# Moving the last down-projection gradient slab to the end of a fused forward and backward kernel, with other orders at its start

## The chip, the cores and the metric

The kernel runs as one program on one core of a Trainium2 chip. The metric is device time in microseconds (us) of one execution. Five runs of the kernel before are given, and one more execution under the hardware profiler, whose views are read here. TensorE does the matrix multiplications, VectorE and ScalarE work element by element, GpSimd mostly issues transfers, and SyncE does nothing else. The views call them PE, DVE, ACT, POOL and SP.

## The reference

The input `x` has 2048 rows of 1024 columns. The output is `x + s * g`, with two branches on the normalized rows, and the kernel returns the output and nine gradients.

```python
xn = _layernorm(x)
k_shift = sum(k_pad[t:t+S] * shift_k[:, 3-t])      # four taps
kv = k_shift * v
y = irfft(rfft(kv, 2S) * rfft(ssm_k, 2S))[:S]      # long convolution
y = y + kv * ssm_D
s = xn * y
h = (xn @ w_gate) * (xn @ w_up)                    # 1024 -> 3584
g = silu(h @ w_down)                               # 3584 -> 1024
out = x + s * g
_out, _vjp = jax.vjp(_f, x, k, v, shift_k, ssm_k, ssm_D, w_gate, w_up, w_down)
```

## The kernel before

**Tiles.** The 2048 rows are 16 blocks of 128. The 3584 hidden columns are 14 slabs of 256 (`NSL`, `SLW`). Matrix multiplications accumulate in PSUM, from where ScalarE or VectorE takes them out. The 1024 channels of the convolution are 8 groups of 128 (`ds`) or 4 pairs (`dp`).

**Order.** The program is recorded by a layer that keeps the order of the statements mostly, hoists what has a higher priority, and inserts the waits. Every engine then works through a fixed list, so an instruction that waits holds back what stands behind it on its engine. That holds for the issue of transfers too: SP and POOL have one list each. `tc.issue_after` keeps an instruction behind another one. `make_pump` runs a second stream of work (a generator which yields estimated costs) in pieces between the matrix multiplications, up to a given fraction.

**The stages, by time in the profile.**

1. Start, to about 86 us. `layer_norm` (L533) normalizes six chunks of rows (1, 1, 2, 4, 4 and 4 blocks), mostly on VectorE. The transposed rows go to `XNT`. `gu_unit` (L604) multiplies one chunk with one slab of the gate and up weights: PSUM `psg` (two buffers), then ScalarE's copy `gut` (L618), then on VectorE `hN = gate * up`, then transposes (L636) and `hT`. The order of the first units is a list in the loop over `xs`: units 0 to 3 do slab 0 and then slab 1 of their chunk. In the same loop the four taps of the shift are turned on ScalarE (`turn_taps`, L150, two at a time), spread to all partitions through memory (`WTd`, `Wbc`), and the sine tables are built (`build_tables`, L168, transposes L190, copies to `TI` L191).
2. To about 548 us. The other slabs of the units, with the forward convolution (`conv_forward`, L645) pumped between them. It loads shifted `k` rows and `v` (`load_kv`), multiplies by the taps (`shift`), transposes filter rows loaded by `load_h` (L692 and L694), transforms (L231), multiplies spectra and transforms back.
3. To about 744 us. `h @ w_down` (L1102) and the gate (`gate`, L1107).
4. To about 1368 us. Per slab: `dh` (L1233) and the gradients of the gate and up weights (L1250), with the convolution's gradient (`conv_backward`, L939, beginning with `dy_forward`, L916) pumped between.
5. To 1570 us. The gradient of `w_down`: for each slab `k` a matrix of 256 by 1024, 64 multiplications of 128x512 with depth 2048 (L1353), ScalarE's copies (L1355) and stores. In between SP issues loads for stage 6: transposed weights `WGU` (`load_wgu`, L1314, 14 pieces) and transposed gradients `dgut` (`load_dgut`, L1316, 14 pieces for four blocks of rows). For k = 13 piece 5 is loaded, pieces 6 to 13 follow after that slab's last store.
6. To the end. `dx`: for every block of rows 14 parts (`dx_part`, L1373) of 8 multiplications (L1376), then `ln_backward` (L1393): add the other branch's gradient, two ScalarE passes with row sums into `dx_t` (L1405, L1407), the correction, and the store of `out_1`. `dx_t` has one buffer. Blocks 0 to 3 are done together, then pairs; blocks 14 and 15 one by one, block 15 in two halves of columns. Pumped into this (L1380) is `dk_units` (L1039): 16 units for the gradients of `k` and the taps. A unit takes seven VectorE operations of about 0.7 us and four of about 1.2 us (L1081), and SP loads two transposed tiles for it, `kT` (L1053) and `dkT` (L1055), each with one buffer.

Of the kernel before, what the change touches and what calls it, by code (L numbers as in the profile page):

```python
# [19 lines left out]
def build_kernel(  # L20
# [147 lines left out]
    def build_tables(psp, tg, ang):  # L168

        m = ang  # L170
        for q in range(2):
            dst = T4[q].rearrange("p r k f -> p k r f")
            sc = 2.0 * np.pi / 4096.0
            mm = tg.tile([P, 8, P], I32, name="mm")
            if q == 0:
                V.tensor_single_scalar(mm[:], m[:], 4095, ALU.bitwise_and)
            else:
                nc.gpsimd.iota(mm[:], pattern=[[512 * q, 8], [0, P]], base=0, channel_multiplier=0)
                tt(mm[:], m[:], mm[:], ADD)
                V.tensor_single_scalar(mm[:], mm[:], 4095, ALU.bitwise_and)  # L180
            nc.scalar.activation(dst[:, 1], mm[:], ACT.Sin, bias=negpi[:], scale=sc)
            ab_ = tg.tile([P, 8, P], F32, name="ab_")
            nc.scalar.activation(ab_[:], mm[:], ACT.Abs, bias=negpi[:], scale=sc)
            nc.scalar.activation(dst[:, 0], ab_[:], ACT.Sin, bias=mhpi[:], scale=1.0)
        for j in range(2):
            for rq in range(2):
                ps = psp.tile([P, 4, 2, P], BF16, name="tr")
                for i in range(4):
                    for k in range(2):
                        nc.tensor.transpose(ps[:, i, k, :], T4[j][:, 4 * rq + i, k, :], ident[:])  # L190
                V.tensor_copy(TI[:, j, 4 * rq:4 * rq + 4], ps[:])  # L191
# [320 lines left out]
    for i in range(52):  # L512
        nc.tensor.matmul(ps[:, i % 4, :], ident[:], ident[:], start=True, stop=True)

    bsb = pool("bc_sb", 1)
    tg = pool("tg", 1)
# [128 lines left out]
    def conv_forward():  # L645
        cx = pool("cx", 1)
        cs = pool("cs", 1)
        kst = pool("kst", 1)
        S_ = {}

        def load_kv(dp, c):
            v = U[4][:, 2048 * c:2048 * c + 2048].rearrange("p (a x) -> p a x", a=8)
            cld_v(v, c, dp * 256, 256)
            k = kst.tile([P, 2, 11, P], BF16, name="k", bufs=2)
            for e in range(2):
                cld_k(k[:, e], c, 2 * dp + e)
            S_["kv", dp, c] = (k, v)

# [45 lines left out]
        def tail(ds):  # L704
            G = S_.pop(("G", ds))
            yf = cs.tile([P, NB, P], BF16, name="yf")
            for rp in range(4):
# [5 lines left out]
                yield  # L713

        load_h(0)
        with tc.issue_after(xsts[4].ins):
            load_kv(0, 0)
            load_kv(0, 1)
        def half(ds, x, i, first=None):
# [70 lines left out]
        for _ in tl:  # L790
            yield 1.0
        kst.release()
        cs.release()
        cx.release()

    F_TOTAL = 4 * 20.0 + 6.0 + 8 * (0.5 + FWD4_W + 1.3 + PROD_W + INV_W) + 10.0 - 0.95 * 8 * (4 * 1.75 + 0.95 + 4 * 0.9)
    F_TOTAL += len(EIGHT) * 2 * (FWD8_W - 9.6 + 0.95 * 1.75) - 2.0
    chunks = [(0, 1), (1, 1), (2, 2), (4, 4), (8, 4), (12, 4)]
    xs = [(b0, n, u8((4, 6, 7)[b0 // 4 - 1], a=4) if n == 4 else lnp.tile([P, n, D], BF16, name=f"x{b0}")[:])
# [20 lines left out]
    for i, (b0, n, x4) in enumerate(xs):  # L820
        if i + 1 < len(xs):
            with tc.issue_after(last.ins):
                last, root, xst = layer_norm(*xs[i + 1])
            xsts.append(xst)
        if i in (2, 3):
            with tc.issue_after(act_copy[0].ins):
                for j in (2 * i - 4, 2 * i - 3):
                    turn_taps(j)
        if i == 3:
            with tc.issue_after(xsts[-1].ins):  # L830
                spread_taps()
        for i_, sl in ([(i, 0), (i, 1)] if i < 4 else ([(4, 0)], [(5, 0), (4, 1), (5, 1)])[i - 4]):
            gu_unit(sl, *xs[i_][0:2], slabs[sl], nop)
        if i == len(xs) - 1:
            with tc.issue_after(root.ins), tc.issue_after(last.ins):
                build_tables(ps_st, tg, ang)
    st(RSd.rearrange("(c u r) -> u c r", c=2, u=P), RSTD[:].rearrange("u (c r) -> u c r", c=2))
# [4 lines left out]
    ps_cv = pool("ps_cv", 2, space=PSUM)  # L842
    pump, drain = make_pump(conv_forward(), F_TOTAL)
    cnt = [0]
# [71 lines left out]
    def dy_forward(xs_, sp, cs, then):  # L916
# [10 lines left out]
        load(1)  # L927
        yield 4.0
        half(0, 0)
# [162 lines left out]

    C_TOTAL = 4.0 + 8 * FWD8_W + 16 * (PROD_W + INV8_W) + 8 * 1.4 + 8 * 2.5
    bpump, bdrain = make_pump(conv_backward(), C_TOTAL)

# [220 lines left out]
    def load_dgut(g, n):  # L1316
# [5 lines left out]
        return t  # L1322

    flush()
    ts = []
    for k in range(NSL):
        if k + 2 < NSL:
            load_h(k + 2)
# [13 lines left out]
        if k == 12:  # L1342
            load_wgu(6, gw.tile([P, 4, D], BF16, name="W1")[:])
            ts.append(load_dgut(0, 4))
        if k == 13:
            ts.append(load_dgut(0, 5))
        h = hs.pop(k)
        for f in range(2):
            wbs = wo.tile([P, D], BF16, name="wbs")[:]
            for dh in range(2):  # L1350
                ps = ps_b.tile([P, 512], F32, name="psb")
                for b in range(NB):
                    nc.tensor.matmul(ps[:], h[:, b, f * P:(f + 1) * P], DBM[b // 4][:, b % 4, dh * 512:(dh + 1) * 512],  # L1353
                                     start=(b == 0), stop=(b == NB - 1))
                nc.scalar.copy(out=wbs[:, dh * 512:(dh + 1) * 512], in_=ps[:])  # L1355
# [16 lines left out]

    def dx_part(t, i, ps, n, dhs=(0, 1)):  # L1373
        for f in range(4):
            for dh in dhs:
                nc.tensor.matmul(ps[:, dh * 512:(dh + 1) * 512], t[n][:, f, i * P:(i + 1) * P],  # L1376
                                 WGU[n][:, f, dh * 512:(dh + 1) * 512],
                                 start=(n == 0 and f == 0), stop=(n == 13 and f == 3))
        kcnt[0] += 1
        kpump(kcnt[0] / (14.0 * 14))  # L1380

    ln_in = {}

    def ln_loads(b):
        rows = slice(b * P, (b + 1) * P)
        ts_ = []
        for nm_, src in (("dxna_t", DXNAd), ("xn_t", XNd), ("dout_t", grad_out.flatten_outer_dims())):
            t = gl.tile([P, D], BF16, name=nm_, bufs=1)
            cld(t[:], src[rows, :])
            ts_.append(t)  # L1390
        ln_in[b] = ts_

    def ln_backward(b, mm, parts=1):  # L1393

        rows = slice(b * P, (b + 1) * P)
        dxna_t, xn_t, dout_t = ln_in.pop(b)
        dxn = gl.tile([P, D], F32, name="dxn", bufs=1)
        prod = gl.tile([P, D], F32, name="prod", bufs=1)
        dx_t = gl.tile([P, D], BF16, name="dx_t", bufs=1)
        cols = [slice(h * D // parts, (h + 1) * D // parts) for h in range(parts)]  # L1400
        sums = gs.tile([P, 2, 2], F32, name="sums")
        for h, cl in enumerate(cols):
            ps = mm(h)
            tt(dxn[:, cl], ps, dxna_t[:, cl], ADD)
            nc.scalar.activation(dx_t[:, cl], dxn[:, cl], ACT.Identity, accum_out=sums[:, 0, h:h + 1])  # L1405
            tt(prod[:, cl], dxn[:, cl], xn_t[:, cl], MUL)
            nc.scalar.activation(dx_t[:, cl], prod[:, cl], ACT.Identity, accum_out=sums[:, 1, h:h + 1])  # L1407
        if parts == 2:
            tt(sums[:, :, 0], sums[:, :, 0], sums[:, :, 1], ADD)
        negm = gs.tile([P, 2], F32, name="negm")  # L1410
        pinned(V.tensor_scalar(negm[:], sums[:, :, 0], -1.0 / D, None, op0=MUL))
        for cl in cols:
            nc.scalar.activation(prod[:, cl], xn_t[:, cl], ACT.Identity, bias=negm[:, 0:1], scale=negm[:, 1:2])  # L1413
            tt(dxn[:, cl], dxn[:, cl], prod[:, cl], ADD)
            pinned(V.scalar_tensor_tensor(dx_t[:, cl], dxn[:, cl], RSTN[:, b:b + 1], dout_t[:, cl], op0=MUL, op1=ADD))  # L1415
            if parts == 1:
                ln_loads(b + 1)
            (st if parts == 1 else ld)(out_1.flatten_outer_dims()[rows, cl], dx_t[:, cl])

    for n in range(6, 14):  # L1420
        with tc.issue_after(wst.ins):
# [10 lines left out]
    for i in range(4):  # L1432
# [5 lines left out]
        with tc.high_priority(40):  # L1438
            ln_backward(i, lambda h: pss[i][:])
    for g in range(1, 4):  # L1440
        for b in (4 * g, 4 * g + 2):
            if b == NB - 2:
                break

            pss = [ps_x.tile([P, D], F32, name="psx") for i in range(2)]
            for n in range(14):
                for i in range(2):
                    dx_part(ts, b % 4 + i, pss[i], n)
                if b % 4 == 2:
                    ts[n] = load_dgut(g + 1, n)  # L1450
            for i in range(2):
                with tc.high_priority(40):
                    ln_backward(b + i, lambda h: pss[i][:])
    for b in (NB - 2, NB - 1):
        parts = 2 if b == NB - 1 else 1

        def mm(h):
            ps = ps_x.tile([P, D], F32, name="psx")
            for n in range(14):
                dx_part(ts, b % 4, ps, n, (h,) if parts == 2 else (0, 1))  # L1460
            return ps[:, h * 512:(h + 1) * 512] if parts == 2 else ps[:]
        ln_backward(b, mm, parts)
    kdrain()
    for p_ in (ps_x, kw_, gs, gl, gd2, ub, ua, gd, gw):
# [64 lines left out]
```

## Time and profile before

| what | value |
|---|---|
| five runs: median (lowest to highest) | 1979.06 us (1961.16 to 1982.79) |
| profiled execution: time | 1975.54 us |
| profiled execution: span, first to last instruction | 1973.8 us |
| outside the span | 1.7 us |
| PE busy | 1924.1 us, 97% of the span |
| DVE busy | 1525.5 us, 77% |
| last matrix multiplication of the program | starts near 1960.5 us |
| mean speed, all transfers | 225 GB/s |

The busy time of PE is near the span, so what PE does not fill (about 50 us) is what a new order can move. It has two sorts: waits of PE inside the stages, and the stretch after its last matrix multiplication.

### The profile page before, as it was taken

To read this page: it belongs to the slowest core of one execution; us is meant where nothing else is said; L and a number is where in the kernel's file an instruction comes from. 1 tells how busy PE (TensorE), PEld (TensorE's weight loads), DVE (VectorE), ACT (ScalarE), POOL (GpSimd) and SP (SyncE) were. 2 spreads that over 40 slices of the span, in tenths; PEclk is the share of its full clock that TensorE was granted. 3 is DMA by queue.
4 is the path that set the end of the run, shared out by engine and by line. 5 is a ranking of instruction groups with operands and counts; after the bars stand their busy time and mean duration, and the time that the engine had idled before them with its cause. 6 is when DMAs were issued, how large, how long until landed. Compare 5 with 4: busy or idle time off the path is not lost.

```text
span 1973.8 us, 27333 instructions
## 1 busy us (share of the span) xinstructions
PE 1924.1 (97%) x10907; PEld 1039.4 (53%) x11043; DVE 1525.5 (77%) x1716; ACT 642.2 (33%) x945; POOL 361.3 (18%) x528
## 2 busy tenths in 40 slices
PE   8999999999999998999999999999999999999997
PEld 4555555555444446666556666664444444444443
DVE  8799999999636554888898989999986332666665
ACT  5655555555422234333222222221212101111113
POOL 3413122111112220000122122021212000111111
PEclk9999999999999999999999999999999999999998
DMA  8968667557799988566778778575898999999892
GB/s 283 304 218 271 230 221 262 193 181 254 258 288 287 292 279 271 182 219 207 258 238 275 235 228 284 193 269 178 163 267 215 145 190 218 188 171 179 170 170 77
DMA packets 452271, 444.43 MB, mean 225 GB/s; under 512 B 282656, under 2 KB 370536, under 8 KB 438192
## 3 DMA queue, kind: packets, MB, share of 16 engines
q1 hardware_dynamic: 390976, 228.93, 47.1%
q0 software_dynamic: 44848, 184.39, 28.6%
q10 hardware_dynamic: 16320, 29.36, 4.0%
q8 instruction: 86, 1.41, 0.3%
q14 instruction: 41, 0.34, 0.1%
HBM read 194.00 MB, written 189.84 MB: 194 GB/s over the span
## 4 chain that ended last, share of the span: by engine, by line
PE 59%; issue 14%; DVE 10%; DMA 9%; POOL 3%; SPq 3%; ACT 2%; another core or an unknown queue 0%; POOLq 0%; DVEq 0%; ACTq 0%
PE psb L1250 19%; PE psg L616 11%; PE psb L1233 9%; PE psb L1353 8%; PE psbm L1102 3%; DMA out_dram<-dx_t 3%; PE psx L1376 3%; PE psF L231 2%; DVE dkp L1081 2%; SPq L1314 1%; DVE dxn L209 1%; DMA U<-Hd 1%; DVE dka L209 1%; ACT prod L1413 1%; DVE dx_t L1415 1%
## 5 line engine op out<-in xcount | busy, mean ns | idle before, releaser
L616 PE MATMUL psg<-wslab,U 128*128 128x512 bf16 x1732 | 404.3, 381 | 9.8 <-ACT gut L618 3.4
L1250 PE MATMUL psb<-U,U 128*128 128x512 bf16 x1792 | 397.2, 379 | 0.0
L1376 PE MATMUL psx<-U,dgut 128*128 128x512 bf16 x1504 | 331.7, 379 | 4.9 <-DMA dgut<-DGd 2.6
L1376 PEld LDWEIGHTS <-dgut 128*128 128x128 bf16 x1792 | 175.0, 98 | 215.5 <-DMA dgut<-DGd 4.7
L1250 PEld LDWEIGHTS <-U 128*128 128x128 bf16 x1792 | 175.2, 98 | 197.7
L616 PEld LDWEIGHTS <-U 128*128 128x128 bf16 x1792 | 173.6, 98 | 195.8 <-issue 7.4
L1233 PE MATMUL psb<-wdt,U 128*128 128x256 bf16 x1792 | 206.8, 273 | 1.1 <-ACT bm L1120 1.1
L1353 PE MATMUL psb<-U,U 128*128 128x512 bf16 x875 | 193.4, 379 | 1.4 <-DMA U<-Hd 0.3
L1233 PEld LDWEIGHTS <-U 128*128 128x128 bf16 x1792 | 175.9, 98 | 32.4 <-issue 1.4
L618 ACT CAST gut<-psg 128x512 bf16<-128x512 f32 x216 | 126.4, 587 | 181.3 <-PE psg L616 165.4
L1102 PE MATMUL psbm<-U,ht 128*128 128x512 bf16 x768 | 168.9, 379 | 0.8
L1255 ACT CAST wb<-psb 128x512 bf16<-128x512 f32 x112 | 65.7, 587 | 311.9 <-PE psb L1250 300.9
L209 DVE TENSOR_TENSOR W<-W 128x1024 f32<-128x1024 f32 (+1 forms) x150 | 151.3, 1026 | 3.1
L1353 PEld LDWEIGHTS <-U 128*128 128x128 bf16 x896 | 87.4, 98 | 105.1 <-DMA U<-Hd 0.8
L1405 ACT ACTIVATE dx_t<-dxn 128x1024 bf16<-128x1024 f32 (+1 forms) x17 | 17.1, 1007 | 334.6 <-DVE dxn L209 243.3
L1102 PEld LDWEIGHTS <-ht 128*128 128x128 bf16 x784 | 76.6, 98 | 91.8
L209 DVE TENSOR_TENSOR U<-U,dht 128x2048 bf16<-128x2048 bf16 x56 | 68.4, 1223 | 51.4 <-ACT dht L1235 51.2
L1235 ACT CAST dht<-psb 128x512 bf16<-128x512 f32 x112 | 65.7, 587 | 120.4 <-PE psb L1233 118.2
L1081 DVE SCALAR_TENSOR_TENSOR dkp<-dkT,kT 128x1024 bf16<-128x1024 bf16 (+2 forms) x64 | 78.4, 1225 | 19.4 <-DMA dkT<-DKSHd 17.6
L1355 ACT CAST wbs<-psb 128x512 bf16<-128x512 f32 x56 | 32.8, 587 | 160.1 <-PE psb L1353 144.8
L209 DVE TENSOR_TENSOR W<-SP 128x1024 f32<-128x1024 f32 x64 | 74.3, 1220 | 3.4 <-ACT SP L253 2.5
L209 DVE TENSOR_TENSOR HX<-W 128x1024 bf16<-128x1024 f32 (+3 forms) x65 | 74.0, 1188 | 0.4
(229 smaller groups left out, 2322.7 us busy)
## 6 DMA issues: line engine op xcount, KB each, us to landing
U<-GUd SPq DMA_DIRECT2D x28, 1024.0 KB, 7.8
DGd<-U SPq DMA_DIRECT2D x28, 1024.0 KB, 4.8
GUd<-gut ACTq DMA_DIRECT2D x54, 512.0 KB, 6.0
out_dram<-wb SPq DMA_DIRECT2D x112, 128.0 KB, 3.8
U<-Hd SPq DMA_DIRECT2D x14, 1024.0 KB, 6.8
Hd<-hN POOLq DMA_DIRECT2D x54, 256.0 KB, 4.8
HTd<-hT POOLq DMA_DIRECT2D x54, 256.0 KB, 3.1
ht<-HTd SPq DMA_DIRECT2D x7, 1536.0 KB, 9.7
```

Of the source, the lines that this page charges most:

```text
L209: pinned(V.tensor_tensor(o, a, b, op))
L231: mm = nc.tensor.matmul(ps[:, k].rearrange("p (c d) -> p c d", c=2), T[:, r, k, :], xr[:, r], start=(n == 0), stop=(n == len(rs) - 1 and ( ...
L616: gu_mm[0] = nc.tensor.matmul(ps[:], XNT[q][:, dc, qi * P:(qi + 1) * P], w[:, dc].rearrange("p a f -> p (a f)"), start=(dc == 0), stop=(dc ...
L618: nc.scalar.copy(out=gut[:, :, i], in_=ps[:].rearrange("p (a f) -> p a f", a=2))
L1081: ins = V.scalar_tensor_tensor(prod[:].rearrange("p r d -> p (r d)")[:, lo:H], dkT[:, 0, lo:H], 1.0, kT[:, 0, 13 + m + lo:13 + m + H], op0 ...
L1102: nc.tensor.matmul(ps[:, dh * 512:(dh + 1) * 512], ht(fc)[:, i * P:(i + 1) * P], WD[fc // 4][:, fc % 4, dh * 512:(dh + 1) * 512], start=(f ...
L1233: nc.tensor.matmul(ps[:, x * SLW:(x + 1) * SLW], DBMT[2 * hf + g][:, dc, (b % 4) * P:(b % 4 + 1) * P], wdt[:, dc, :], start=(dc == 0), sto ...
L1235: nc.scalar.copy(out=dht[:, 2 * e:2 * e + 2].rearrange("p b f -> p (b f)"), in_=ps[:])
L1250: nc.tensor.matmul(ps[:], XN[b // 4][:, b % 4, dc * P:(dc + 1) * P], dgus[b // 8][:, :, b % 8], start=(b == 0), stop=(b == NB - 1))
L1255: nc.scalar.copy(out=wb[:, dc % 2].rearrange("p a f -> p (a f)"), in_=ps[:])
L1353: nc.tensor.matmul(ps[:], h[:, b, f * P:(f + 1) * P], DBM[b // 4][:, b % 4, dh * 512:(dh + 1) * 512], start=(b == 0), stop=(b == NB - 1))
L1376: nc.tensor.matmul(ps[:, dh * 512:(dh + 1) * 512], t[n][:, f, i * P:(i + 1) * P], WGU[n][:, f, dh * 512:(dh + 1) * 512], start=(n == 0 and ...
```

## The change

The arithmetic is the same in every stage; what moves is when it is done.

- **End.** The loop of stage 5 does 13 slabs. The last slab's 64 multiplications (now the function `dwd_mm`) come after the `dx` of block 15, into buffers of `ps_x`. Its inputs are loaded again while blocks 14 and 15 are worked on: four pieces of `DBM` and one of `Hd`, issued by SP. Blocks 14 and 15 are now a pair like the others, whose last two parts are done for 14 and then for 15. Block 15 is no longer split, and it has tiles of its own (`own`), in the memory of `dgut` pieces 0 to 5. `dx_t` has two buffers for the other blocks. Piece 5 of `dgut` joins the loads after the last store.
- **Late tap gradients.** The pump of `dk_units` takes 17% of its work over the first 56 parts (blocks 0 to 3) and the rest over the next 126; before, it was even over 196 parts.
- **Start.** The units in the loop over `xs` are (0,0); then (1,0), (0,1), (1,1); then (2,0), (2,1), and so on, as (chunk, slab). The taps are turned one chunk earlier. The first two `load_kv` are issued inside this loop, for chunks 3 and 4, each with `k` ahead of `v`. The copies of the tables go through the one buffer of `ps_y` instead of four of `ps_st`.
- **Backward convolution.** The first step of `dy_forward` is given 7.0 units of the pump instead of 4.0.

```diff
@@ build_tables
-                ps = psp.tile([P, 4, 2, P], BF16, name="tr")
+                ps = psp.tile([P, 4, 2, P], BF16, name="psY")
@@ conv_forward
         def load_kv(dp, c):
-            v = U[4][:, 2048 * c:2048 * c + 2048].rearrange("p (a x) -> p a x", a=8)
-            cld_v(v, c, dp * 256, 256)
             k = kst.tile([P, 2, 11, P], BF16, name="k", bufs=2)
             for e in range(2):
                 cld_k(k[:, e], c, 2 * dp + e)
+            v = U[4][:, 2048 * c:2048 * c + 2048].rearrange("p (a x) -> p a x", a=8)
+            cld_v(v, c, dp * 256, 256)
...
+        load_kv(0, 0)
+        yield 0.0
+        load_kv(0, 1)
+        yield 0.0
+        cx = pool("cx", 1)
+        cs = pool("cs", 1)
         load_h(0)
-        with tc.issue_after(xsts[4].ins):
-            load_kv(0, 0)
-            load_kv(0, 1)
@@ start
-        if i in (2, 3):
+        if i in (1, 2):
             with tc.issue_after(act_copy[0].ins):
-                for j in (2 * i - 4, 2 * i - 3):
+                for j in (2 * i - 2, 2 * i - 1):
                     turn_taps(j)
-        if i == 3:
+        if i == 2:
             with tc.issue_after(xsts[-1].ins):
                 spread_taps()
-        for i_, sl in ([(i, 0), (i, 1)] if i < 4 else ([(4, 0)], [(5, 0), (4, 1), (5, 1)])[i - 4]):
+        if i in (3, 4):
+            with tc.issue_after(xsts[4].ins):
+                next(conv)
+        for i_, sl in ([(0, 0)], [(1, 0), (0, 1), (1, 1)], [(2, 0), (2, 1)], [(3, 0), (3, 1)], [(4, 0)], [(5, 0), (4, 1), (5, 1)])[i]:
             gu_unit(sl, *xs[i_][0:2], slabs[sl], nop)
...
-                build_tables(ps_st, tg, ang)
+                build_tables(ps_y, tg, ang)
@@ dy_forward
-        yield 4.0
+        yield 7.0
@@ down gradient
+    def dwd_mm(ps, h, f, dh):
+        for b in range(NB):
+            nc.tensor.matmul(ps, h[:, b, f * P:(f + 1) * P], DBM[b // 4][:, b % 4, dh * 512:(dh + 1) * 512],
+                             start=(b == 0), stop=(b == NB - 1))
-    for k in range(NSL):
-        if k + 2 < NSL:
+    for k in range(NSL - 1):
+        if k + 2 < NSL - 1:
             load_h(k + 2)
...
-        if k == 13:
-            ts.append(load_dgut(0, 5))
@@ dx
-        kpump(kcnt[0] / (14.0 * 14))
+        kpump(0.17 * kcnt[0] / 56.0 if kcnt[0] <= 56 else 0.17 + 0.83 * (kcnt[0] - 56) / (14.0 * 9))
...
+            dx_t = gl.tile([P, D], BF16, name="dx_t", bufs=2)
+        else:
+            dxn, prod, dx_t = own("dxn", F32, 3), own("prod", F32, 4), own("dx_t", BF16, 5)
...
-    for n in range(6, 14):
+    for n in range(5, 14):
...
-            if b == NB - 2:
-                break
+            end = b == NB - 2
             pss = [ps_x.tile([P, D], F32, name="psx") for i in range(2)]
-            for n in range(14):
+            for n in range(12 if end else 14):
                 for i in range(2):
                     dx_part(ts, b % 4 + i, pss[i], n)
+                if end and n < 4:
+                    DBM[n] = u8((7, 0, 1, 9)[n], a=4)
+                    ld(DBM[n], DBMd[512 * n:512 * n + 512, :].rearrange("(b u) d -> u b d", u=P))
+                if end and n == 4:
+                    h = u8(2, "p (b f) -> p b f", b=NB)
+                    ld(h, Hd[NSL - 1])
...
+            if end:
+                kdrain()
             for i in range(2):
+                if end:
+                    for n in (12, 13):
+                        dx_part(ts, b % 4 + i, pss[i], n)
                 with tc.high_priority(40):
-                    ln_backward(b + i, lambda h: pss[i][:])
-    for b in (NB - 2, NB - 1):
-        parts = 2 if b == NB - 1 else 1
...
-    kdrain()
+                    ln_backward(b + i, pss[i][:])
+    for f in range(2):
+        ps = ps_x.tile([P, D], F32, name="psx")
+        wbs = kw_.tile([P, D], BF16, name="wbs", tag=("dka", "dkp")[f])
+        f0 = (NSL - 1) * SLW + f * P
+        for dh in range(2):
+            hs_ = slice(dh * 512, (dh + 1) * 512)
+            dwd_mm(ps[:, hs_], h, f, dh)
+            nc.scalar.copy(out=wbs[:, hs_], in_=ps[:, hs_])
+            ld(o_dwd[f0:f0 + P, hs_], wbs[:, hs_])
```

## The prediction, made before the changed kernel ran

> **What bounds the kernel.** I read the page's first part, then who PE waited for, then PE's own timeline at its waits, and last the chain that ended last.
>
> ```profile
> PE 1924.1 (97%) x10907; PEld 1039.4 (53%) x11043; DVE 1525.5 (77%) x1716; ACT 642.2 (33%) x945; POOL 361.3 (18%) x528
> PE psF L231 <- DMA A<-DYd: 4.8, 1, 4.8
> PE tr L692 <- DMA U<-in_A_ssm_k_dram: 3.6, 1, 3.6
> PE psg L616 <- ACT gut L618: 3.4, 3, 2.2
> PE tr L580 <- DVE U L569: 3.3, 3, 2.0
> PE psg L616 <- DMA wslab<-in_B_w_gate_dram: 2.7, 1, 2.7
> PE psx L1376 <- DMA dgut<-DGd: 2.6, 3, 1.8
> ```
>
> PE is the bound nearly everywhere, so only PE's idle time can be won: some 27 us of waits, and the stretch behind its last multiplication. Here is that stretch, from PE's timeline and the chain (start, length, what).
>
> ```profile
> 1954.88 5.99 PE L1376 MATMUL psx<-U,dgut 128*128 128x512 bf16 x27
> ...
> 1960.41 3.21 DMA out_dram<-dx_t
> ...
> 1963.70 0.07 ACT dx_t L1405
> ...
> 1969.95 0.75 DVE dx_t L1415
> ```
>
> PE ends at 1960.9 and the span at 1973.8, 12.9 us later. Block 15's first ScalarE pass starts at 1963.7, because the one `dx_t` waits for block 14's store (3.2 us). The last VectorE result is ready at 1970.7, its store lands at 1972.4, closing instructions take 1.4: 3.1 us from result to end.
>
> **The end of the program.** Stage 5 loses the 64 multiplications of slab 13. Back to back such a one takes 0.216 us (32 start within 6.9 us), so 13.8 us of PE leave there and come back behind block 15: nothing saved in PE's sum. What changes is what lies behind PE's last multiplication.
> - After: last multiplication, ScalarE's copy (0.59, L1355), store and closing (3.1 as above): 3.7 us.
> - Beside it runs the rest of `ln_backward`. An undisturbed one takes 7.8 us on VectorE (blocks 12's: 1930.6 to 1938.4). Block 14 is ready 16 multiplications (3.5 us) before the end of `dx`; two in a row end 12.2 us behind it, with a POOL store (3.2) and the closing (1.4) 16.8. PE's path needs 13.8 + 3.7 = 17.5, so PE sets the end, by 0.7 us. ScalarE's first `wbs` copy stands ahead of block 15's passes, but is ready sooner than they are.
>
> Gain 12.9 - 3.7 = **9.2 us**. The cover is the reload: SP issues 5 MB behind the parts of blocks 14 and 15. One MB of `Hd` landed in 5.5 us at 1513, so 27 us. The first can go at part 0, 3.5 us into the pair, and they are needed 48.3 us into it: 17 us to spare. I take nothing; if they started only where the pair ends, 27 us.
>
> **The dx stage, begun 13.8 us earlier.** Its loads do not move with it by themselves; this is SP's list (a row can stand for several issues):
>
> ```profile
> 1557.85 1.56 SPq L1053 DMA_TRANSPOSE kT<-in_A_k_dram  x1
> ...
> 1589.62 1.16 SPq L1053 DMA_TRANSPOSE kT<-in_A_k_dram  x1
> ...
> 1593.40 3.01 SPq L1321 DMA_TRANSPOSE dgut<-DGd  x2
> ```
>
> Pieces 6 to 13 stand behind four `kT`/`dkT` pairs. Each pair waits until VectorE has finished the unit before (some 10 us: seven operations of 0.7, four of 1.2). From 1593.4 to the landing of piece 13 (1657.6) are 64.2 us, and PE waited there twice (0.25 and 0.57), then 1.79 for the next group's piece 12. In the changed order three pairs stand ahead, then pieces 5 to 13. The first pair came after the load of `Hd` for slab 13 and piece 5; both are gone, so it can be issued where piece 5 was, at about 1550.4. `dkT` lands near 1556.5, unit 0 ends at 1561.5, unit 1 at 1571.5, piece 5 is issued near 1574.5. With 3.0 for it, piece 13 lands near 1641.7. PE begins `dx` at 1557 and needs piece 13 at 1557 + 49 x 1.73 = 1641.8. So these loads are just in time, as before; half of 0.8 saved. The next group's loads stand without a pair between pieces 11 and 12 (2.6 us of issuing), so 1.8 goes too, and with `Hd` 0.27. Gain **2.5 us**; bounds -2.9 and +7 (the pairs at their old times). The even pump was 1/196 per part; now it is slower, then 0.83/126, 29% faster. VectorE then has 13.3 units (135 us) and twelve `ln_backward` (94) in 217 us: late by about 12 us, behind which stand only later `kT` pairs and `dgut` loads with a pair of blocks (48 us) to spare.
>
> **The start.** PE's timeline, and VectorE's row that holds up the third chunk:
>
> ```profile
> 13.65 0.39 PE L616 MATMUL psg<-wslab,U 128*128 128x512 bf16 x1 [2.68 <-DMA wslab<-in_B_w_gate_dram]
> 17.89 0.29 DVE L209 TENSOR_TENSOR hN_s<-gut_s 128x256 bf16<-128x256 bf16 x1 [3.02 <-ACT gut_s L618]
> 41.60 1.51 PE L580 MATMUL tr<-ident,U 128*128 128x128 bf16 x24
> 52.04 0.98 PE L580 MATMUL tr<-ident,U 128*128 128x128 bf16 x8 [2.00 <-DVE U L569]
> 53.67 2.41 PE L580 MATMUL tr<-ident,U 128*128 128x128 bf16 x24
> ```
>
> Unit (0,1) waits for slab 1's gate half; its product holds VectorE for 3.0 us; from then VectorE works without a gap to 53 us, and PE waits for its last chunk at 52. In the new order chunk 1's transposes come first (its rows are ready at 11.7), then (1,0), and (0,1) when slab 1 is there. Chunk 2's statistics then wait for (1,0)'s copy near 17.3 instead of the product at 20.1: VectorE is 2.7 us earlier. PE: from 13.8 it has 32.6 us of work up to the last chunk's transposes. Turning two taps (2.1 us on ScalarE) now stands ahead of copies that free `psg`, twice, and makes PE wait about 1.3 and 1.1; it arrives near 49.6 instead of 52.0. That is **-2.4**.
>
> Then the clock. The 24 transposes take 2.41 instead of 1.51 after the 2.00 us wait; the granted clock was a half for 3.4 us here, as from 14.6 to 18.0. The Trainium skill (TensorE: Matmul & The Clock Gate, Part 1, and HAM oscillation) gives half speed after about 3.4 us without work, and asks only that no gap be longer; by it the 2.00 us wait would cost 2.00, and its removal no more. The rows show half speed after 2.0 idle out of 3.4, so 1.7 us more. I take the rows: **-1.7**, sum for this part 4.1 (2.4 by the rule). Ends: all five waits and both slow windows, -9.7; only the taps' waits, +2.4.
>
> Tables through one buffer: at worst each of three rounds waits a VectorE operation (1.23) and a copy (0.62), +5.5; at best the 0.71 now waited goes. Multiplications (0.86) stand between the rounds: 0. Loads of `k` and `v` move from 48-76 us to about 41-55, so `shift` can fill the 7 us which VectorE idles at 57. The skill says (DMA: Bandwidth & Descriptors, Issuing engines are not separate DMA queues) that POOL's transfers share the 16 engines with SP's, which speaks against this: 2.5 MB at the 280 GB/s of the first 50 us is 9 us of all. By the rule the gain is nil. But SP has nothing to move from 31 us, when `copy_k(0)` landed, to 70, and nobody on PE waits for POOL's stores then; and they leave the time at 70-92, when slab 2 and the second copy of `k` are moved. POOL waits 7.6 us for that copy, then issues the filter rows for which PE waits 3.6. Ends 0 and -5.3 (with a slow window); I take **-2.0**.
>
> **Backward convolution.** 3 more units put 16 multiplications of 256 columns (1.75 us) ahead of the first use of `A`, which waited 4.8: **-1.8**; ends 0 and -8.2 (the wait, and 6.8 us at half clock behind it).
>
> **Sum.** 9.2 + 2.5 + 4.1 + 2.0 + 1.8 = 19.6 us: 1975.5 - 19.6 = 1955.9. The profiled execution was 3.5 below the runs' median; carried over, 1959.5. I forecast between them, **1958**.
>
> **Rivals.**
> - *More at the start* (0.12): all waits and slow windows go, and the filter rows are in time. For: they hang on one 2.7 us wait. Against: taps and VectorE stay busy. 5.6 more at the chunks, 3.3 at the filter rows, 3.4 of `A`'s half clock: 1946.
> - *The start gives nothing* (0.18): ScalarE's taps and the table rounds eat it: +6.1, 1964.
> - *Late pieces* (0.13): the transfer stop from 1527 to 1551 (16 GB/s in 1540-1550) lasts longer or the `kT` pairs keep their old times, and piece 13 is 7 us late. 1965.
> - *Slower* (0.05): the reload. `DBM` stands behind the last `kT` pair in SP, that waits for unit 14 on VectorE, which now carries 29% more per part beside `ln_backward`. Before, the taps ended 30 us ahead of `dx`'s end; so kept, the pair goes 40 ahead, and 27 are needed: 12 to spare. Every us later is one of PE idle in front of slab 13. From 32 us on the kernel is slower than before; at 45, 1991.
> - *It does not do what it says* (0.02): same work, same waits, 1976.
>
> **How the numbers follow.** The forecast's case has 0.50, with 1946 to 1964. A measurement of this kernel tells about 1% (19.8 us) from no change; two thirds of that case lie beyond it. Faster 0.34 + 0.12 = 0.46; slower 0.05; the rest 0.49. The range leaves out some 0.1 below and 0.1 above: 1942 to 1971.
>
> **What would show it.** Right: PE's last group is slab 13 with no wait before it, and 3.7 us behind; no wait for `wslab` at the start, PE at the last chunk's transposes near 49.6, no half clock there; `A` waits 3 us. Wrong: waits of slab 13 for `U<-DBMd` or `U<-Hd`; of `psx` for `dgut` over 3 us; new waits of `psg` for `gut` at 20 to 33 us.

## The result, and the profile after

| | median | lowest to highest | runs |
|---|---|---|---|
| before | 1976.54 us | 1961.16 to 1995.75 us | 46 |
| changed | 1964.03 us | 1954.21 to 1967.98 us | 27 |

The ratio is 0.993, with a 95% interval of 0.9913 to 0.9947: 13.8 us faster (10.5 to 17.2; the two medians differ by 12.5), inside what was called "within 1%". The profiled execution took 1960.9 us, with a span of 1959.1 (before: 1973.8).

First the page's busy times and the list of who PE waited for (total us, times, longest) in the changed kernel:

```profile
PE 1922.4 (98%) x10907; PEld 1037.9 (53%) x11043; DVE 1524.0 (78%) x1711; ACT 641.2 (33%) x940; POOL 358.0 (18%) x529
PE psg L617 <- ACT gut L619: 5.1, 3, 2.1
PE psx L1383 <- DMA dgut<-DGd: 4.0, 2, 3.9
PE psg L617 <- ACT gut_s L619: 2.0, 2, 1.1
PE psg L617 <- ACT U L583: 1.9, 1, 1.9
PE psF L231 <- ACT SP L253: 1.8, 1, 1.8
...
PE psF L231 <- DVE kv L209: 1.4, 1, 1.4
```

PE's busy time fell by only 1.7 us, as it should: no multiplication was removed. Read the names rather than the sums. The waits for `A<-DYd` (4.8), the filter rows (3.6) and `wslab` (2.7) are gone; in their place stand waits for ScalarE's `gut`, `gut_s` and `U`, for `SP` and for `kv`, which the list of before did not have or had shorter. `dgut` has become longer.

The end of the program, from the timeline (start, length, engine, line, what; in brackets the idle time before it):

```profile
1940.85 10.52 PE L1332 MATMUL psx<-U,U 128*128 128x512 bf16 x47
...
1950.41 0.56 ACT L1479 CAST wbs<-psx 128x512 bf16<-128x512 f32 x1
...
1951.40 0.59 ACT L1479 CAST wbs<-psx 128x512 bf16<-128x512 f32 x1 [0.43 <-PE psx L1332]
1951.80 1.28 DVE L1422 SCALAR_TENSOR_TENSOR dx_tl<-dxnl,RSTN,dout_tl 128x1024 bf16<-128x1024 f32 x1
1952.04 3.40 PE L1332 MATMUL psx<-U,U 128*128 128x512 bf16 x15 [0.67 <-ACT wbs L1479]
...
1955.69 0.59 ACT L1479 CAST wbs<-psx 128x512 bf16<-128x512 f32 x1 [3.70 <-remote]
```

Slab 13 is PE's last group and no load holds it up. PE's multiplications end at 1955.4, and from there it is ScalarE's last copy, its store and the closing: 3.7 us. Block 15's last VectorE result (`dx_tl`, ready at 1953.1) is earlier, so PE's path sets the end.

### The profile page after: what moved, and what is told of

The parts are those of the page before. It is cut to its first block, busy times and chain, and to the rows that moved or that the text cites. A ratio compares the mean times of both kernels' runs of the same rounds, so it can differ in the third digit from the quotient of the medians.

```text
span 1959.1 us, 27343 instructions
## 1 busy us (share of the span) xinstructions
PE 1922.4 (98%) x10907; PEld 1037.9 (53%) x11043; DVE 1524.0 (78%) x1711; ACT 641.2 (33%) x940; POOL 358.0 (18%) x529
## 3 DMA queue, kind: packets, MB, share of 16 engines
q0 software_dynamic: 44928, 184.65, 28.2%
## 4 chain that ended last, share of the span: by engine, by line
PE 73%; issue 15%; POOL 4%; DMA 3%; DVE 3%; SPq 1%; ACT 1%; another core or an unknown queue 0%; POOLq 0%; ACTq 0%; DVEq 0%
PE psb L1256 19%; PE psx L1383 18%; PE psb L1332 9%; PE psb L1239 9%; PE psg L617 9%; PE psbm L1108 3%; PE psF L231 2%; DMA dgut<-DGd 1%; SPq L1327 1%; DMA HTd<-hT 1%; PE psY L443 1%; POOL HTd L66 1%; DVE W L209 1%; POOL Hd L66 1%; PE psY L1036 1%
## 5 line engine op out<-in xcount | busy, mean ns | idle before, releaser
L617 PE MATMUL psg<-wslab,U 128*128 128x512 bf16 x1732 | 405.0, 381 | 12.6 <-ACT gut L619 5.1
L1256 PE MATMUL psb<-U,U 128*128 128x512 bf16 x1792 | 397.4, 379 | 0.0
L1332 PE MATMUL psb<-U,U 128*128 128x512 bf16 x813 | 179.6, 379 | 1.0
L1415 ACT ACTIVATE dx_t<-dxn 128x1024 bf16<-128x1024 f32 x15 | 15.9, 1059 | 327.8 <-DVE dxn L209 319.8
L209 DVE TENSOR_TENSOR dxn<-psx,dxna_t 128x1024 f32<-128x1024 f32 x15 | 18.3, 1223 | 89.7 <-PE psx L1383 84.0
```

Source lines behind the costliest of these rows:

```text
L209: pinned(V.tensor_tensor(o, a, b, op))
L617: gu_mm[0] = nc.tensor.matmul(ps[:], XNT[q][:, dc, qi * P:(qi + 1) * P], w[:, dc].rearrange("p a f -> p (a f)"), start=(dc == 0), stop=(dc ...
L1256: nc.tensor.matmul(ps[:], XN[b // 4][:, b % 4, dc * P:(dc + 1) * P], dgus[b // 8][:, :, b % 8], start=(b == 0), stop=(b == NB - 1))
L1332: nc.tensor.matmul(ps, h[:, b, f * P:(f + 1) * P], DBM[b // 4][:, b % 4, dh * 512:(dh + 1) * 512], start=(b == 0), stop=(b == NB - 1))
```

## The experiments

Each kernel below is a part of the change. Their profiles matter as much as their times, since they are six executions of shared code: three with the old start and three with the new one, four with yield 4.0 and two with 7.0, three with the old end and three with the new one.

**1. Only the end.**

```diff
-    for k in range(NSL):
+    for k in range(NSL - 1):
...
-        kpump(kcnt[0] / (14.0 * 14))
+        kpump(0.17 * kcnt[0] / 56.0 if kcnt[0] <= 56 else 0.17 + 0.83 * (kcnt[0] - 56) / (14.0 * 9))
...
-        dx_t = gl.tile([P, D], BF16, name="dx_t", bufs=1)
+            dx_t = gl.tile([P, D], BF16, name="dx_t", bufs=2)
...
+    for f in range(2):
...
+        for dh in range(2):
...
+            dwd_mm(ps[:, hs_], h, f, dh)
```

> Only the end of the change: slab 13 held back, blocks 14 and 15 as a pair with tiles of block 15's own, dx_t in two buffers, the late tap gradients. Start and yield 4.0 as before. Theory A (sections of the two profiles): stretch behind the last multiplication of slab 13's kind 12.9 -> about 4.5 us, -8.4; dx stage +3.4 because the next group's last dgut pieces come late: sum -5 us (ratio 0.9975). Rival B (the sum in the prediction): -9.2 and -2.5, so -11.7 us (ratio 0.994). In the profile A expects a wait psx <- dgut of 3 us or more at the end of block 3; B expects none over 1 us.

Measured: 1966.28 us against 1974.33 of before, ratio 0.9978 (0.9951 to 1.0004). That is 4.3 us (a gain of 9.7 to a loss of 0.8): theory A's 5 lies near the middle, rival B's 11.7 outside, and no change at all just inside. (The medians differ by 8.0, which is still less than B's figure.) In the profile the stretch from the last `dx` multiplication to the end is 18.5 us with slab 13's 13.8 in it, so 4.7, as in the whole change. The `dgut` waits are there, but not as A put them: four of them, 4.2 us in all and 1.5 at most, near 1880 to 1894, in the last group of four blocks and not the second. A had expected one of 3 us or more, B none over 1 us.

**2. Only the start.**

```diff
-        for i_, sl in ([(i, 0), (i, 1)] if i < 4 else ([(4, 0)], [(5, 0), (4, 1), (5, 1)])[i - 4]):
+        for i_, sl in ([(0, 0)], [(1, 0), (0, 1), (1, 1)], [(2, 0), (2, 1)], [(3, 0), (3, 1)], [(4, 0)], [(5, 0), (4, 1), (5, 1)])[i]:
...
-        if i in (2, 3):
+        if i in (1, 2):
...
-        with tc.issue_after(xsts[4].ins):
-            load_kv(0, 0)
-            load_kv(0, 1)
...
-                build_tables(ps_st, tg, ang)
+                build_tables(ps_y, tg, ang)
```

> Only the start of the change: units in the new order, taps a chunk earlier, load_kv earlier with k first, copies of the tables through psY. Yield 4.0 and the end as before. Theory A (sections of the two profiles): up to the first table transposes +0.6, filter rows in time -4.9, new waits for SP L253 and kv L209 +3.2: sum -1.1 us (ratio 0.9995). Rival B (the prediction): -4.1 and -2.0, so -6.1 us (ratio 0.997). A expects PE at the first table transposes at 86 to 87 us, B at 82.

Measured: 1976.59 us, ratio 1.0011 (0.9988 to 1.0033). Rival B's 0.997 is excluded; A's 0.9995 is inside. The first table transposes began at 84.7 us, earlier than A thought, and 85.2 to 87.8 is what the old start gives. The profiled execution itself was long (span 1981.1) for a reason that the start has no part in: its `dx` stage waited 9.6 us for `dgut`.

**3. Only the yield.**

```diff
-        yield 4.0
+        yield 7.0
```

> Only yield 7.0 in place of 4.0 in dy_forward. Theory A: the wait of psF for A<-DYd (4.8 us) and the 6.8 us at half clock behind it (3.4 lost) go together: -8.2 us (ratio 0.9959). Rival B (the prediction): only the 1.75 us of three units more go: -1.8 us (ratio 0.999), a wait of 3 us stays and the half clock with it.

The pump's total, `C_TOTAL`, grows by the same 3.0. Measured: 1973.90 us, ratio 0.9996 (0.9974 to 1.0017), so by the time alone rival B's 1.8 us stands and A's 8.2 is excluded. By the profile, the wait behaves as A said: none for `A`, no half clock there. Both were half right. The 8.2 us were one execution's price: with 4.0 the same wait took 4.8, 3.6, 3.3 and 3.7 us (before and experiments 1, 2 and 4), and the time at half clock beside it was 6.8, 3.4, 3.4 and 6.8 us.

**4. The whole change without the yield.**

```diff
-        yield 7.0
+        yield 4.0
```

> The whole change but with yield 4.0 as before. Theory A: the wait for A<-DYd and its half clock come back: 8.2 us slower than the changed kernel, that is ratio to before 0.9975 instead of 0.993. Rival B: they were a matter of transfers that other parts of the change have moved, or of the one execution: 0 to 1.8 us slower than the changed kernel, ratio 0.993 to 0.994.

Measured: 1967.93 us, ratio 0.9968 (0.9942 to 0.9994). The wait came back. From the timelines of experiments 1, 2 and 4, in this order:

```profile
772.16 1.87 PE L231 MATMUL psF<-A,TF 128*128 128x256 bf16 x8 [3.56 <-DMA A<-DYd]
```

```profile
769.85 1.40 PE L231 MATMUL psF<-A,TF 128*128 128x256 bf16 x8 [3.26 <-DMA A<-DYd]
```

```profile
773.63 1.86 PE L231 MATMUL psF<-A,TF 128*128 128x256 bf16 x8 [3.72 <-DMA A<-DYd]
```

All three have yield 4.0, and all three wait. The same instruction with 7.0, in the changed kernel and in experiment 3, has no idle time before it:

```profile
768.76 1.03 PE L231 MATMUL psF<-A,TF 128*128 128x256 bf16 x8
```

```profile
772.29 1.04 PE L231 MATMUL psF<-A,TF 128*128 128x256 bf16 x8
```

So the yield is what removes it, and no other part. Its price in time is less sure: 0.9968 against 0.993 says some 7 us (1 to 14), experiment 3 alone says 0.8 (a gain of 5 to a loss of 3). The two intervals share 1 to 5. (The changed kernel's runs belong to another set than those of the experiments, with a median of 1976.54 for before where theirs is 1974.33. The medians of the changed kernel and of experiment 4 differ by 3.9 us.)

**The parts side by side.** Six profiles, cut where PE does the same instruction in each: the first transposes of the tables, PE's last wait of stage 2 (for `hT`), the first multiplication of stage 4, the first of `dx`, the last of `dx`, the end. Where slab 13 is held back, its 13.8 us are added to the fourth column and taken from the last, so that columns compare.

| kernel (parts of the change in it) | to tables | to end of stage 2 | to stage 4 | to `dx` | `dx` | to the end |
|---|---|---|---|---|---|---|
| before (none) | 86.0 | 461.3 | 196.5 | 827.4 | 389.3 | 13.3 |
| 1 (end) | 85.2 | 461.9 | 196.5 | 824.3 | 391.5 | 4.7 |
| 2 (start) | 84.7 | 460.4 | 196.5 | 826.0 | 400.9 | 12.5 |
| 3 (yield) | 87.8 | 461.5 | 196.5 | 821.7 | 389.4 | 9.9 |
| 4 (start, end) | 89.2 | 459.3 | 196.5 | 825.8 | 393.3 | 4.7 |
| changed (all) | 86.6 | 458.9 | 196.5 | 819.8 | 392.6 | 4.7 |

Means with a part against means without it: start +0.5 to the tables and -2.0 behind them; yield -5.1; end -1.7 up to `dx` (the three old ends wait 0.3, 1.3 and 1.8 us for `U<-Hd` there, the new ones not at all), -0.7 in `dx` (+3.2 by medians, since experiment 2's 400.9 pulls the mean) and -7.2 behind it. The sum is -16.4 us, or -12.4 with the medians for `dx`, beside the 13.8 of the timed runs and the 14.7 of the two spans; each row is one execution, and its waits are a sample. The three parts timed alone come to only -2.9 together, with intervals of 4 to 5 us on each: roughly 8 for the sum. By their medians they come to -6.2, against -12.5 for the whole. Both are less than the whole, by about as much as the uncertainties explain. Whether the parts help each other is not settled by these runs.

## Why the prediction was right, and where its steps were not

It said 1958 with a range of 1942 to 1971; it came out 1964 and within 1%. Part of that is luck. It gave "within 1%" 0.49 and "faster" 0.46, nearly a coin toss: seen from the median of all 46 runs before, "faster" begins at 1956.8, only 1.2 us below its own number. And of its five gains, 19.6 us in all where 13.8 were measured, only the end had the place right and the size near. The filter rows had the size by another route, the start and the `dx` stage gave nothing, and the backward convolution made up for part of them with 3.3 us more than it was given.

Of the signs that it named, those for the end came true, and PE ran at full clock at the last chunk. `A` was to wait 3 us and does not wait. Two of its signs of being wrong came too: a wait for `dgut` over 3 us (3.9), and waits of `psg` at 20 to 33 us (1.1 at 22.3 and 0.9 at 33.3). The latter are the taps' waits, which its own sum contains, so as a sign they could not tell.

**The start: -4.1 predicted, +0.5 measured.** The rival that the start gives nothing was right in that, but not in why: it blamed the taps and the table rounds, and the taps cost what the prediction had already taken off, the rounds nothing on PE. That the kernel then took the rival's 1964 is chance, since the other terms moved too. Up to the last chunk the mechanism held: its transposes begin at 50.4, 49.9 and 53.3 us in three executions against 52.0, 52.1 and 53.9, so 1.5 us earlier on the mean. (2.4 was predicted, from a work sum that is itself loose: 13.8 + 32.6 + 1.3 + 1.1 is 48.8, and the text says 49.6.) The wait for `wslab` is not gone for good: experiment 4, with the same start, waits 1.9 and 1.4 us for it. The taps' two waits are 1.1 and 0.9 us in the changed kernel (1.3 and 1.1 predicted). Two terms failed.

- A wait that the sum did not have stands at 14.75 us: ScalarE's `gut_s` of the first unit is now ahead of the copy of chunk 1's transposes (`U`, L583), and PE waits 1.9, 1.7 and 1.9 us for it.
- Behind the last chunk the gain is lost again. This is the chain from the changed kernel's timeline:

```profile
63.33 1.17 POOL L66 DMA_DIRECT2D RSTN<-RSd  x1 [2.56 <-DMA RSd<-RSTD]
64.50 1.03 POOL L178 IOTA mm<- 128x1024 int32 x1
65.56 1.23 DVE L209 CUSTOM_DVE_ANT_0 mm<-m,mm 128x2048 uint16<-128x2048 uint16 x1 [1.81 <-POOL mm L178]
67.83 0.69 DVE L180 TENSOR_SCALAR mm<-mm 128x1024 int32<-128x1024 int32 x1
68.56 1.15 ACT L181 ACTIVATE TF<-mm,negpi 128x1024 bf16<-128x1024 int32 x1 [2.79 <-DVE mm L180]
70.23 5.30 PE L617 MATMUL psg<-wslab,U 128*128 128x512 bf16 x16 [2.10 <-ACT gut L619]
```

Read it from top to bottom: each line waits for the one above. GpSimd waits 2.56 us for a small transfer to land (`RSd`) before it can issue the next (`RSTN`); the iota for the second table stands behind that in GpSimd's list; VectorE waits for the iota, and takes one operation of the shift before its second step (L180); ScalarE waits for VectorE, and PE for a `gut` behind ScalarE's sine. Before, iota (63.45) stood ahead of `RSTN` (65.43), but VectorE lost that lead again to a wait of 1.07 us for `k`, and did the second step at 67.93. So the second table is no earlier than it was (67.83), while PE comes to it 2.2 us earlier (64.5 instead of 66.7) and has to wait. In experiment 2 the chain is the same:

```profile
62.12 1.16 POOL L66 DMA_DIRECT2D RSTN<-RSd  x1 [2.55 <-DMA RSd<-RSTD]
64.35 1.22 DVE L209 CUSTOM_DVE_ANT_0 mm<-m,mm 128x2048 uint16<-128x2048 uint16 x1 [1.23 <-POOL mm L178]
67.34 1.15 ACT L181 ACTIVATE TF<-mm,negpi 128x1024 bf16<-128x1024 int32 x1 [2.77 <-DVE mm L180]
69.02 1.89 PE L617 MATMUL psg<-wslab,U 128*128 128x512 bf16 x8 [2.07 <-ACT gut L619]
```

Experiment 4 has it too (2.47 us on PE). Together with the next wait for `gut`, PE loses 2.1, 2.9 and 3.3 us here with the new start, and 0.8, 1.2 and 2.0 with the old one. A wait for `gut` behind the first table's sine, near 59, 58 and 62 us, is new as well (0.9, 0.3 and 1.0). The two make the 2 us by which PE falls back. The step that failed is the one that stopped at the last chunk: it did not follow GpSimd's list and the tables' chain into the changed order. That putting iota first would give some 1.5 us back is argued, not tried.

**The half clock at the start: -1.7 predicted.** The row on which this was built did not repeat. The 2.0 us wait for the last chunk is in all three executions of the old start; half clock followed it in one. With the new start it is found at other waits: behind 2.1 us at 30.2 in experiment 4 and behind 2.1 us at 70.2 in the changed kernel.

**Filter rows: -2.0 predicted, -2.0 measured, but by another route.** The wait for `in_A_ssm_k` (3.6, 2.0 and 1.4 us with the old start) is gone in all three executions with the new one. PE stood 4.9 us earlier behind it. Most of that is given back at two waits, `SP` L253 (1.76) and `kv` (1.42). Here is why, from VectorE's timeline, the start of a stretch and the last `kv` of the pair, before:

```profile
95.80 4.63 DVE L209 TENSOR_TENSOR W<-SP 128x1024 f32<-128x1024 f32 x4 [2.48 <-ACT SP L253]
191.50 1.22 DVE L209 TENSOR_TENSOR kv<-U,U 128x2048 bf16<-128x2048 bf16 x1
```

and after:

```profile
95.25 4.63 DVE L209 TENSOR_TENSOR W<-SP 128x1024 f32<-128x1024 f32 x4 [3.13 <-ACT SP L253]
190.95 1.23 DVE L209 TENSOR_TENSOR kv<-U,U 128x2048 bf16<-128x2048 bf16 x1
```

Between the two rows VectorE works without a gap, in all six executions (the next idle time over 0.15 us comes behind 263 us), and takes the same 95.7 us. So it is only 0.55 us earlier, and PE, which needs that `kv`, cannot gain more. The old start shows the exchange as well: where the filter rows cost 3.6, 2.0 and 1.4 us, the wait for `kv` was 0, 0.2 and 1.8. The filter rows were the wait that showed; VectorE was close behind. Counted from the tables, VectorE begins that stretch at 8.6 us with the new start instead of 9.5 to 9.8, and that gives about half of the gain; which of the reorderings did it was not separated.

**Tables through one buffer: nothing predicted.** Right for PE: it waits 0.5 to 0.7 us for the copies `TI` in the three executions with four buffers, and not at all in the three with one. VectorE does wait 0.7 us for PE at each of two rounds, which it did not before.

**Backward convolution: -1.8 predicted, -5.1 measured.** The cover was counted right: from the first multiplication of stage 4 to the first use of `A` PE now has 26.8 us of work instead of 25.0. The prediction subtracted 1.75 from a wait of 4.8 and left 3 us. The term that was wrong is the arrival: relative to that first multiplication `A` landed at 29.7, 28.5, 28.2 and 28.7 us with 4.0, and at 26.8 and 26.3 with 7.0. Issue is at 15.8 to 16.2 us in all six. So the load came 1.4 to 3.4 us sooner, and wait and half clock went together. In the changed kernel that is just enough: `A` lands within 0.1 us of its use. Why it comes sooner is open. Until 24.6 us behind the mark all six executions run the same instructions at the same times and issue the same transfers in the same order, so no transfer that was moved explains it. What the traces do show is that a load issued 1.4 us earlier, the transposed `wdt`, shares the change (16.1 to 17.5 us from issue to landing with 4.0, 14.0 and 14.7 with 7.0), and that the DMA engines are full and move little while it is under way: in the kernel before, from 18 to 26 us behind the mark, a mean busy share of 1.29 moves 91 GB/s, where 1.00 moved 406 in the 4 us ahead of that. With two executions against four, chance is not excluded.

**The dx stage: -2.5 predicted, +3.3 between the two profiles.** The first half held, with more room than I gave it; SP's list in the changed kernel:

```profile
1541.24 1.54 SPq L1059 DMA_TRANSPOSE kT<-in_A_k_dram  x1
...
1562.69 1.17 SPq L1059 DMA_TRANSPOSE kT<-in_A_k_dram  x1
...
1566.34 6.48 SPq L1327 DMA_TRANSPOSE dgut<-DGd  x4
...
1659.81 31.03 SPq L1327 DMA_TRANSPOSE dgut<-DGd  x9
1690.93 1.48 SPq L1059 DMA_TRANSPOSE kT<-in_A_k_dram  x1
```

The first pair goes at 1541.2 and piece 5 at 1566.3, 9 and 8 us ahead of the prediction, as PE's own start of `dx` is (1548.0). Piece 13 landed at 1627.3 and PE did not wait for it. "So 1.8 goes too" is what failed here: no pair stands between the next group's pieces 11 and 12, just as I said, and yet

```profile
1687.92 28.62 PE L1383 MATMUL psx<-U,dgut 128*128 128x512 bf16 x122 [3.88 <-DMA dgut<-DGd]
```

The row of SP with nine transposes shows the reason: 31.0 us for nine, 3.4 each, where undisturbed ones are issued every 1.3 us. Two of them took 7.4 and 8.6 us to be issued, and they landed 22 and 16 us after that instead of 4 to 5. GpSimd's loads and stores beside them took 14 to 17 us as well. It was the transfers that were slow, not the list. In these stretches (length, busy times and counts of PE, PEld, DVE, ACT, POOL, granted clock, mean busy share of the DMA engines, GB/s) they are full and move less:

```profile
1640.00:1662.00 22.00, 21.89 (x102) 9.94 (x103) 13.37 (x14) 7.09 (x10) 4.85 (x9) 1.00 1.20 232
1662.00:1690.00 28.00, 23.86 (x105) 10.39 (x106) 16.45 (x23) 3.55 (x5) 6.07 (x10) 0.97 1.17 160
```

What falls together there is the same in all three kernels with the new end: 116 to 118 us into `dx` GpSimd issues the store and the load of a tap gradient unit (`dka`, `dkh`) beside the loads of `ln_backward`, and the next pieces of `dgut` take up to 22.0, 16.4 and 12.6 us to land (changed kernel, experiments 1 and 4). With the old end no unit falls into 105 to 128 us, and no piece issued from 110 to 130 us is seen to take over 10.8. In the changed kernel alone PE had to wait for one.

Nor was a lateness of about 12 us safe, with "a pair of blocks (48 us) to spare". In two of the three kernels with the late tap gradients the last group waits; SP's list and PE's rows in experiment 4:

```profile
1833.04 6.61 SPq L1327 DMA_TRANSPOSE dgut<-DGd  x3
1847.01 1.19 SPq L1059 DMA_TRANSPOSE kT<-in_A_k_dram  x1
...
1849.64 14.04 SPq L1327 DMA_TRANSPOSE dgut<-DGd  x6
1863.77 1.24 SPq L1059 DMA_TRANSPOSE kT<-in_A_k_dram  x1
...
1873.01 11.40 PE L1383 MATMUL psx<-U,dgut 128*128 128x512 bf16 x52 [1.64 <-DMA dgut<-DGd]
1887.47 32.08 PE L1383 MATMUL psx<-U,dgut 128*128 128x512 bf16 x140 [3.07 <-DMA dgut<-DGd]
```

SP idles from 1839.6 to 1847.0 in front of a pair that VectorE is late to release, then issues without a pause and does not catch up. Experiment 1 waits there too (4.2 us); no kernel with the even pump does. They wait in the first two groups instead, and the changed kernel in the second. Over the stage it is 2.6, 2.3 and 9.6 us with the old pump, 4.0, 4.2 and 4.7 with the new one: the waits were moved, not removed. An even pump in the changed kernel was not tried, so that the pump is the cause is argued, not shown.

**The end: -9.2 predicted, -7.2 measured.** The side after is right to 1 us: 18.5 us from the last `dx` multiplication against 17.5, of which 0.67 is the wait in front of the last 16 multiplications that the sum left out (they wait for ScalarE's copy of the other half of the same `psx` tile). Behind PE's last multiplication are 3.7, 3.4 and 3.4 us (3.7 predicted). The reload was issued from 1896.1 to 1910.0 and had landed by 1922.0, 19 us before slab 13 (17 predicted), so the slower rival had no ground. What was mis-sized is the side before: the 12.9 us came from one execution, and two others of the same code have 12.1 and 9.5. In all three block 15's first pass waits for the store of block 14 out of the one `dx_t`. In two of them that wait ends behind PE's last multiplication and so lengthens the end. In experiment 3 the store was issued at 1949.0 instead of 1960.4, and the wait was over while PE was still at work:

```profile
1951.01 6.21 PE L1376 MATMUL psx<-U,dgut 128*128 128x512 bf16 x28
1952.18 0.63 ACT L1405 ACTIVATE dx_t<-dxn 128x512 bf16<-128x512 f32 x1 [6.58 <-DMA out_dram<-dx_t]
```

How much the second buffer of `dx_t` alone would have given was not tried.

## What to carry to other kernels

When two waits stand one behind the other on the same engine, price the removal of the first by the second: follow every engine of the changed order to the next point where they meet, including the one that "only issues transfers". A wait of 2 to 5 us for a transfer is a sample, not a constant; where the same code is in several profiles, take the spread of the wait and not its one value, for the gain and for the stretch that the gain is subtracted from. And look for the engine that works without a gap in a stretch: here VectorE's 95.7 us, and not PE's wait for the filter rows, said what could be won. Loads that are just in time can stay so when their consumer moves: here moving other work moved the place of the wait for `dgut` and did not shorten it.

## What the runs showed of the hardware

How closely the spread of one kernel goes with the granted clock was new to me. Over 35 runs of the kernel before, the mean granted clock ran from 0.989 to 0.998 and the time with it: a line through them rises 2.5 us for each 0.001 of clock missing (correlation -0.82 between clock and time). The two runs at 0.990 took 1984.6 us on the mean, the one at 0.998 took 1965.6. Not all of it is the clock's doing: 0.001 of 1974 us is 2.0 us of lost work, and half clock comes with waits, which cost time of their own. The changed kernel's runs lie between 0.997 and 1.000 and scatter less (a standard deviation of 4.0 us instead of 6.0). The idle stretch behind PE's last multiplication, of which 10.2 us ran at half clock before without cost, is not the reason: experiments 1 and 4 lack it too, go down to 0.990 and 0.992, and scatter by 7 us.

In all six profiles half clock comes in pieces of 3.41 us or twice that, but for the last one, which runs into the end. All 11 waits of PE that were 2.5 us or longer were beside one. Of 18 waits between 1.8 and 2.5 us (behind the first 12 us), 6 were, and the same wait had it in one execution and not in the next. One piece (experiment 2, at 1722.7) stands behind three waits of 1.5, 1.6 and 0.9 us that lie close together. The Trainium skill (TensorE: Matmul & The Clock Gate, What's actually happening) says that the activity window is 3413 ns and runs freely, not started by the program; the lengths here agree, and a window that starts anywhere would explain a 2 us wait that costs 1.7 us more in a third of the executions. Read so, the -1.7 of the prediction was worth about -0.6. Its other statement, half clock after about one idle window of 3.4 us, is too mild for this kernel: 2.5 us were enough each time, in 11 waits.
